# Reordering key and query preparation in a windowed attention plus feed-forward kernel on one Trainium2 core

## The chip, the cores and the metric

One Trainium2 chip (trn2), one core. The metric is the device time of one execution in microseconds (us). TensorE (PE) multiplies, VectorE (DVE), ScalarE (ACT) and GpSimd (POOL) work on its results, SyncE (SP) issues transfers; GpSimd also issues transfers, those that change the number type.

## The reference, cut to what matters

```python
# q, k, v: (4 batches, 8 heads, 768 positions, 64), fp32
k_sum = k.reshape(B, H, 24, 32, D).max(axis=3)        # one key per block of 32
v_sum = v.reshape(B, H, 24, 32, D).mean(axis=3)
scores_l = q @ k.T / 8     # kept where |i - j| < 16
scores_s = q @ k_sum.T / 8 + log(32)
a = softmax(concat(masked scores_l, scores_s))
x = a @ concat(v, v_sum)                              # (3072 tokens, 512)
h = x @ w_in                                          # 512 -> 2048
out = (h * sigmoid(1.702 * h)) @ w_out                # 2048 -> 512
```

## The kernel before, in words

The four batches go through one pipeline. While the feed-forward part of batch b runs on TensorE, the keys, queries and values of batch b + 1 are prepared and its attention is done in the gaps that the plans name. Every instruction of an engine is kept in program order, so the place of a call in the code is its place in the engine's queue.

Attention. For a head pair p (four of them, `NP`), `kx[p][s]` holds the keys turned (head dimension on the partitions), with 16 halo positions on each side and the 24 block keys in every tile of 128; s is the slot, b % 2. `qT` holds the turned queries. `scores(b, half, p)` does 12 products into a two-bank PSUM buffer of the pool `psb` (two buffers, tag "big") and one exponential on ScalarE; `mask(half, p)` multiplies by the window on VectorE; `values` multiplies with the value tile `vw[s]`, whose halos (`halo_dmas`) and block sums (`sum_dmas`, after `vsum` on TensorE and `block_sums` on VectorE) come by transfers within the chip. `norm` writes `x2`; its turned form `xT` feeds the feed-forward part.

Turning is done in two ways. `q_late(p)`, `tk` and `tq` turn on TensorE through PSUM and copy out. For batches 2 and 3, `xk(g, s)` turns two head pairs of keys with two transfers on SP, `xq(g, s)` two pairs of queries with one, `dx(half, g)` the attention result, one of four tiles `xT00` to `xT11`. They all stand in SP's queue, with the stores of the result and the halo and sum transfers.

Loads are issued by GpSimd. `load_turned` loads key or query groups (two transfers each for g = 0 and 1) into `kb` or `qb`, which have two buffers each; `load_batch(b)` issues the keys, 12 value transfers, and the queries (for batch 3 the queries are issued later, behind a small copy `gate2` that makes GpSimd wait for `xT11`). `rest_k` finishes keys: block maxima on VectorE, halos and block keys on VectorE or, out of `tk`, on GpSimd.

Feed-forward. Batch 0 is treated in two halves (`ff_in`, `ff_out`); in `ff_out(0, ...)` twelve slots follow each other and `plan0` names what comes beside each: `q0` to `q3` are `q_late`, `s0` to `s3` are `scores` and `mask` of the second half, `v`, `x` values and turns. Slots of batch 1 (`plan1`) run beside `ff_out(1, ...)`.

From batch 1 on the loop over b runs 16 first-layer steps in eight groups (n // 2 = 0 to 7: products `ph`, an activation on ScalarE, sums `g_sums` on VectorE) and then 21 second-layer products (`seq`, slots i = 0 to 20), seven for each of three token tiles t, with `plan` beside them. `product(b, t, what)` adds into banks A, B and C of the pool `pmm` (four buffers, tag "mm"). Bank A of a tile is kept open over products 1, 6, 7 and 4, and is read in between. Results go to `o1` and `o2` of a tile, taken from the pool `outp` (three buffers), and are stored by SP once written. In batch 1's pass these slots hold, in SP's order: tile 0's two stores, `xT00`, tile 1's `o1`, `xT01`, tile 1's `o2`, `xT10`, `xT11`, then the four key transposes of batch 3, tile 2's stores.

The last batch has a form of its own behind that (`ff_product`, `ff_copy`), which the change does not touch.

Of the kernel before, what the change touches and what calls it, by code (L numbers as in the profile page):

```python
# [35 lines left out]
def kernel(  # L36
# [28 lines left out]
    dve = _Ordered(tc, nc.vector)  # L65
    act = _Ordered(tc, nc.scalar)
# [14 lines left out]
    kb2, qb2 = {}, {}  # L81
# [41 lines left out]
    def load_turned(x, b, t2, name, gs_=(0, 1)):  # L123

        for g in gs_:
            t2[g] = castp2.tile([128, 2, NJ, 2, D], BF16, name=name, tag=name)
            for hh in range(2):
                h0 = hh * NP + 2 * g
                pool.dma_start(out=t2[g][:, :, :, hh].rearrange("p i a d -> p (i a) d"),
                               in_=x[b, h0:h0 + 2].rearrange("h (a p) d -> p (h a) d", p=128))  # L130

    def load_v(b):
        w5 = vw[b % 2].rearrange("p (j e) h c -> p j e h c", e=2)
        src = v[b].rearrange("h (j e p) d -> e j p h d", e=2, p=64)
        for j in range(NJ):
            for e in range(2):
                pool.dma_start(out=w5[e * 64:e * 64 + 64, j, e, :, 0:D], in_=src[e, j])
# [108 lines left out]
    def load_batch(b):  # L246
        if b == 3:
            pool.tensor_copy(out=gate2, in_=qTs[0][:, 0, 0:1])
        load_turned(k, b, kb2, "kb")
        if b == 3:  # L250
            pool.tensor_copy(out=gate2, in_=qTs[0][:, NP - 1, 0:1])
        if b == 1:
            load_turned(q, b, qb2, "qb", (0,))
        load_v(b)
        if b < 3:
            load_turned(q, b, qb2, "qb", (1,) if b == 1 else (0, 1))
# [12 lines left out]
    def copy(eng, out, in_):  # L269
        if eng is act:  # L270
            act.activation(out=out, in_=in_, func=ACT.Copy)
        elif eng == "dve_alone":

            dve.tensor_reduce(out=out, in_=in_.unsqueeze(len(in_.shape)), axis=AX.X, op=ALU.max)
        else:
            eng.tensor_copy(out=out, in_=in_)
# [65 lines left out]
    def at(ap, start, dims):  # L342
        a = ap[:, start:start + 1]
        return bass.AP(tensor=a.tensor, offset=a.offset, ap=[a.ap[0]] + dims)

    def flat_kx(p, s):
        return kx[p][s].rearrange("p t c -> p (t c)")
# [25 lines left out]
    def turn_plain(ps, src):  # L373

        n, rows = src.shape[0], src.shape[2]
        for r in range(rows):
            for h in range(2):
                pe.transpose(out=ps[h * 64:h * 64 + 64, r * n:r * n + n], in_=src[:, h, r],
                             identity=ident[0:n, 0:n])
# [31 lines left out]
    def turn_tiles(ps, src, n):  # L411

        for a in range(n):
            pe.transpose(out=ps[:, a * 128:a * 128 + 128], in_=src[:, a].rearrange("p h d -> p (h d)"),
                         identity=ident)

    def q_late(p, eng):
        if p != 2:
            ps = psb.tile([128, 2048], BF16, name="ps_q", tag="big")
        else:  # L420
            ps = pmm.tile([128, 1024], BF16, name="ps_q", tag="mm")
        turn_plain(ps[:, 0:HALF], qb2["late"][:, 2 * p:2 * p + 2])
        copy(eng, qT[p][0][:, HALF:S].rearrange("p (c r) -> p c r", r=JH),
             ps[:, 0:HALF].rearrange("p (r c) -> p c r", r=JH))
# [130 lines left out]
    def tk(p, s, eng):  # L555
        ps = psb.tile([128, 2048], BF16, name="ps_t", tag="big")[:, 0:S]
        turn_tiles(ps, kb2[p // 2][:, p % 2], NJ)
        copy(eng, at(flat_kx(p, s), 0, [[256, NJ], [192, 2], [1, 64]]),
             ps.rearrange("p (j e c) -> p j e c", e=2, c=64))
        rest_k(p, s, pool)  # L560

    def tq(p, s, eng):
        ps = pmm.tile([128, 1024], BF16, name="ps_t", tag="mm")[:, 0:S]
        turn_tiles(ps, qb2[p // 2][:, p % 2], NJ)
        copy(eng, qT[p][s], ps)

    def xk(g, s):
        k4 = kxs[s].rearrange("p i (j e) c -> p (i j) e c", e=2)
        src = kb2[g].rearrange("p i a h d -> p (i a h d)")
        for e in range(2):  # L570
            sp.dma_start(out=k4[:, 2 * g * NJ:2 * (g + 1) * NJ, e, e * 64:e * 64 + 64],
                         in_=src[e * 64:e * 64 + 64], transpose=True)
# [5 lines left out]
    def rest_k(p, s, eng=dve):  # L578
        ks = attp.tile([128, nb], BF16, name="ks", tag="ks")
        dve.tensor_reduce(out=ks.rearrange("p (j e n) -> p j e n", e=2, n=2),  # L580
                          in_=at(flat_kx(p, s), 0, [[256, NJ], [192, 2], [block, 2], [1, block]]),
                          axis=AX.X, op=ALU.max)
        key_halos(p, s, eng)
        key_rows(p, s, ks, eng)
# [92 lines left out]
    def ff_one(half, nt):  # L677
        ph = pmm.tile([128, HALF], F32, name="ph", tag="mm")
        ff_step(ph, half, nt)
        gelu(half, nt, ph)  # L680
# [13 lines left out]
    def w_sum(what, part):  # L694

        n = NT // 2
        c = slice(part * n // 2, (part + 1) * n // 2)
        w1, w2 = w_out_sb[:, 0:n], w_out_sb[:, n:]
        b11, b12, b21, b22 = w1[:, c, 0:N1], w1[:, c, N1:], w2[:, c, 0:N1], w2[:, c, N1:]
        a, b = {0: (b12, b11), 1: (b22, ws[:, 0, c]), 2: (b22, b12), 3: (b21, ws[:, 1, c])}[what]  # L700
        dve.tensor_tensor(out=ws[:, what, c], in0=a, in1=b, op=ALU.subtract)
# [14 lines left out]
    def win_sum(what):  # L716

        n = NT // 2 * 128
        k1, k2 = w_in_sb[:, K1], w_in_sb[:, K2]
        a11, a12, a21, a22 = k1[:, :, 0:n], k2[:, :, 0:n], k1[:, :, n:], k2[:, :, n:]  # L720
        a, b_, op = {0: (a21, a22, ALU.add), 1: (wsi[0], a11, ALU.subtract),
                     2: (a11, a21, ALU.subtract), 3: (a12, wsi[1], ALU.subtract)}[what]
        dve.tensor_tensor(out=wsi[what], in0=a, in1=b_, op=op)
# [167 lines left out]
    def exp_soon():  # L891
        act.activation(out=gate[:, 1:2], in_=gate[:, 0:1], func=ACT.Exp)
# [134 lines left out]
    load_batch(1)  # L1027


    plan0 = {1: ["q0", "q1", "q2"], 2: ["q3", "s0", "s1"], 4: ["s2", "s3"], 6: ["v0", "v1"], 8: ["x0"], 9: ["x1"]}  # L1030

    plan1 = {-1: ["s00", "s01"], 1: ["t2", "m00", "m01"], 2: ["t3", "s02"], 3: ["s03", "m02"], 4: ["m03", "s10"],
             5: ["s11", "m10"], 6: ["v00", "m11", "s12", "s13"], 7: ["v01", "g"], 8: ["m12", "m13"],
# [41 lines left out]
    def value_rows(s):  # L1075
        w5 = vw[s].rearrange("p (j e) h c -> p j e h c", e=2)
        halo_dmas(w5, 0)
        vsum(s)
        block_sums()
        sum_dmas(w5, 0)  # L1080
# [13 lines left out]
    for i, (ms, part) in enumerate((ms, part) for part in range(4) for ms in range(JH)):  # L1094
        ff_out(0, ms, part)
        beside0(i)
        if i in (10, 11):
# [2 lines left out]

    todo = {3: [lambda: tk(0, 1, act)], 4: [lambda: w_sum(2, 0)], 5: [lambda: tk(1, 1, act)],
            6: [lambda: w_sum(2, 1)], 7: [lambda: w_sum(3, 0)], 8: [lambda: tk(2, 1, act)], 
            10: [lambda: w_sum(3, 1)], 9: [lambda: tq(0, 1, dve)], 11: [lambda: tk(3, 1, act)], 12: [lambda: tq(1, 1, dve)],
            15: [lambda: value_rows(1)]}
    ff_in(1, range(3))
    for nt in range(3, NT):
# [15 lines left out]
    for b in range(1, B - 1):  # L1122
        nxt = b + 1 < B
        s = (b + 1) % 2
        if b == B - 2:
            for w in range(4):
                win_sum(w)
        for n in range(0, NT, 2):
            if n == 0:
                ff_open(order2[0:4], (lambda: tx(1, 1)) if b == 1 else None)  # L1130
            elif n == 2:
                for nt in order2[0:4]:
                    ff_one(1, nt)
                g_sums(0)
                g_sums(1)
            else:
                for nt in order2[n:n + 2]:
                    for half in range(2):
                        ff_one(half, nt)
                g_sums(n // 2, dve, (0, 1) if n + 2 == NT else (0, 1, 2, 3))  # L1140
            if nxt:
                if n == 0 and b > 1:
                    pool.tensor_copy(out=gate2, in_=xTT[1][1][:, 1, 0:1])
                    load_turned(q, b + 1, qb2, "qb")
                if n // 2 == 1:
                    value_rows(s)
                if n // 2 == 2 * b:
                    xq(0, s)
                    xq(1, s)
                if n // 2 in (2, 3, 4, 5):  # L1150
                    rest_k(n // 2 - 2, s)
        if nxt:
            exp_soon()
            beside(b + 1, -1)
        i = 0
        for t, what in seq:
            product(b, t, what)
            if i == 0:
                g_sums(NT // 2 - 1, dve, (2, 3))
            if nxt:  # L1160
                beside(b + 1, i)
            i += 1
            if nxt and b + 2 < B:
                if i == 1:
                    load_batch(b + 2)
                if i in (16, 18):
                    xk(i // 2 - 8, b % 2)

    mid.close()
    for ab in (True, False):  # L1170
# [1 line left out]
    b, n = B - 1, NT // 2  # L1172
# [79 lines left out]
```

## Time and profile before

| | |
|---|---|
| median of 3 runs | 206.19 us (205.59 to 206.76) |
| the profiled execution | 205.72 us |
| its span, first to last instruction | 203.7 us |
| PE busy / weight loads | 196.8 us / 136.7 us |
| DVE / ACT / POOL busy | 141.6 / 125.4 / 90.3 us |
| mean granted TensorE clock | 0.998 |
| moved by transfers | 28.13 MB, mean 138 GB/s |

All times in the views are from the start of the span. A row of a timeline gives start, length, engine, line, operation, what is written and read, a count and, in brackets, the idle time before it and what ended it. All program lines show as L28, a helper, so groups are told apart by the names of their tiles: `ps_q` are query turns of batch 0, `ps_s` scores, `ph` first-layer and `po` second-layer products. SPq and the POOL rows named DMA are the issue of transfers and not the transfers; these are told by their time from issue to landing. In rows of queues q0 is what GpSimd issued and q1 what SP and ACT issued: packets, MB, and the time that the packets took as a share of 16 transfer engines over the stretch (packets overlap, so it can pass 100%).

### The profile page before, as it was taken

How to read it: one execution, taken by the hardware profiler on the slowest of the kernel's cores; microseconds unless marked ns; L12 is line 12 of the kernel's file. 1: busy time of each engine (PE TensorE's matmuls, PEld its weight loads, DVE VectorE, ACT ScalarE, POOL GpSimd, SP SyncE). 2: the span in 40 equal slices, each digit the busy share in tenths (PEclk: the TensorE clock that was granted, in tenths of full speed). 3: DMA queues.
4: the chain of work that ended last, by engine and by line, in shares of the span. 5: the costliest groups of instructions: out<-in, count | busy, mean ns of one | idle time of the engine just before them, and what ended most of it. 6: DMA issues, size and time to landing. Idle time of an engine off the chain costs nothing.

```text
span 203.7 us, 5850 instructions
## 1 busy us (share of the span) xinstructions
PE 196.8 (97%) x2358; PEld 136.7 (67%) x2358; DVE 141.6 (70%) x391; ACT 125.4 (62%) x240; POOL 90.3 (44%) x141
## 2 busy tenths in 40 slices
PE   6899999999999999999999999998999999999993
PEld 6567554556754665665888965666888855668882
DVE  6776885594855874897768689895769567758221
ACT  4674875539777617777871546778580568984220
POOL 7955489456899592002974035000000019870000
PEclk9999999999999999999999999999999999999999
DMA  6999999999999999999999979999022940000223
GB/s 179 159 164 204 207 210 218 184 156 240 107 157 149 185 181 165 139 162 156 118 185 146 154 125 137 130 241 180 0 106 52 172 140 3 0 0 0 106 105 103
DMA packets 95994, 28.13 MB, mean 138 GB/s; under 512 B 83664, under 2 KB 93152, under 8 KB 95968
## 3 DMA queue, kind: packets, MB, share of 16 engines
q0 software_dynamic: 69648, 13.24, 82.1%
q1 hardware_dynamic: 26176, 14.39, 34.9%
q8 instruction: 18, 0.29, 0.6%
q10 hardware_dynamic: 144, 0.13, 0.2%
q14 instruction: 8, 0.07, 0.1%
HBM read 27.26 MB, written 6.29 MB: 165 GB/s over the span
## 4 chain that ended last, share of the span: by engine, by line
PE 82%; DMA 9%; DVE 5%; ACT 1%; issue 1%; SPq 0%; ACTq 0%; DVEq 0%
PE ph L28 23%; PE poA L28 16%; PE po L28 11%; PE poB L28 8%; PE ps_av L28 4%; PE phA L28 4%; DMA out_dram<-osb 4%; PE poC L28 4%; PE ps_s L28 3%; DMA qT<-qb 3%; DMA gT<-in_k_dram 2%; DVE ks L28 2%; PE ps_t L28 1%; PE ps_x L28 1%; DVE qT L28 1%; DVE gs L28 1%
## 5 line engine op out<-in xcount | busy, mean ns | idle before, releaser
L28 PE MATMUL ph<-xT,w_in_sb 128*128 128x384 f16 x400 | 67.6, 326 | 0.1
L28 PEld LDWEIGHTS <-w_in_sb 128*128 128x128 f16 x442 | 42.7, 98 | 27.1 <-issue 0.2
L28 ACT ACTIVATE gT<-ph 128x384 f16<-128x384 f32 x100 | 47.9, 492 | 17.9 <-PE ph L28 17.1
L28 PEld LDWEIGHTS <-gT 128*128 128x128 f16 x312 | 28.8, 98 | 11.0
L28 ACT ACTIVATE a_sb<-ps_s 128x768 bf16<-128x768 f32 (+1 forms) x32 | 25.0, 826 | 12.1 <-PE ps_s L28 12.1
L28 PEld LDWEIGHTS <-gs 128*128 128x128 f16 x288 | 27.7, 98 | 3.4
L28 POOL DMA_DIRECT2D vw<-in_v_dram x36 | 24.6, 704 | 11.2 <-DMA kb<-in_k_dram 4.1
L28 POOL TENSOR_TENSOR gs<-gT 128x384 f16<-128x384 f16 x8 | 7.3, 911 | 43.1 <-PE phC L28 42.0
L28 PE MATMUL po<-w_out_sb,gT 128*128 128x512 f16 x96 | 23.6, 380 | 0.0
L28 DVE TENSOR_TENSOR a_sb<-a_sb,mk 128x768 bf16<-128x768 bf16 x28 | 14.9, 554 | 6.5 <-ACT a_sb L28 5.9
L28 PE MATMUL poA<-ws,gs 128*128 128x256 f16 x144 | 18.7, 273 | 0.0
L28 DVE TENSOR_TENSOR x<-ps_av,rc 128x384 f16<-128x384 f32 x32 | 17.8, 558 | 1.1
L28 DVE TENSOR_TENSOR gs<-gT 128x384 f16<-128x384 f16 (+1 forms) x34 | 13.3, 390 | 7.2 <-ACT gT L28 6.9
L28 POOL DMA_DIRECT2D qb<-in_q_dram x16 | 15.1, 964 | 3.1 <-DMA v0n<-in_v_dram 1.7
L28 PEld LDWEIGHTS <-kx 64*128 64x128 bf16 (+1 forms) x378 | 10.0, 95 | 7.8 <-issue 4.9
L28 DVE TENSOR_REDUCE ks<-kx 128x24 bf16<-128x768 bf16 x12 | 11.4, 948 | 3.4 <-ACT kx L28 3.2
L28 POOL DMA_DIRECT2D kb<-in_k_dram x14 | 13.6, 987 | 0.3 <-issue 0.3
L28 ACT ACT_TABLE_LOAD x10 | 12.8, 1283 | 1.0 <-PEq L1236 0.8
L28 ACT ACTIVATE osb<-poA 128x256 f32<-128x256 f32 x9 | 3.5, 384 | 15.8 <-PE poA L28 15.8
L28 ACT ACTIVATE s<-poA 128x256 f32<-128x256 f32 x11 | 4.2, 385 | 11.2 <-PE poA L28 11.2
L28 PEld LDWEIGHTS <-a_sb 128*64 128x64 bf16 (+2 forms) x400 | 7.8, 108 | 2.8 <-issue 1.3
L28 PE MATMUL poA<-w_out_sb,gT 128*128 128x256 f16 x72 | 9.4, 273 | 0.0
(117 smaller groups left out, 288.9 us busy)
## 6 DMA issues: line engine op xcount, KB each, us to landing
out_dram<-osb SPq DMA_DIRECT2D x22, 256.0 KB, 3.7
kb<-in_k_dram POOLq DMA_DIRECT2D x14, 192.0 KB, 6.6
qb<-in_q_dram POOLq DMA_DIRECT2D x12, 192.0 KB, 10.3
vw<-in_v_dram POOLq DMA_DIRECT2D x36, 64.0 KB, 5.5
w_out_sb<-in_moe_w_out_dram POOLq DMA_DIRECT2D x4, 512.0 KB, 13.0
w_in_sb<-in_moe_w_in_dram POOLq DMA_DIRECT2D x3, 512.0 KB, 12.8
vw<-vs SPq DMA_DIRECT2D x6, 198.0 KB, 6.7
gT<-in_k_dram SPq DMA_DIRECT2D x2, 384.0 KB, 3.5
```

The lines of the kernel that those rows point to most:

```text
L28: r = f(*a, **kw)
```

## The change

Four places move, and no arithmetic changes.

```diff
-        load_turned(k, b, kb2, "kb")
+        load_turned(k, b, kb2, "kb", (1,) if b == 2 else (0, 1))
...
     def q_late(p, eng):
-        if p != 2:
+        if p < 2:
             ps = psb.tile([128, 2048], BF16, name="ps_q", tag="big")
         else:
             ps = pmm.tile([128, 1024], BF16, name="ps_q", tag="mm")
...
-    plan0 = {1: ["q0", "q1", "q2"], 2: ["q3", "s0", "s1"], 4: ["s2", "s3"], ...
+    plan0 = {1: ["q0", "q1", "q2"], 2: ["s0", "s1", "q3"], 4: ["s2", "s3"], ...
...
-            ... 11: [lambda: tk(3, 1, act)], ...
+            ... 11: [lambda: load_turned(k, 2, kb2, "kb", (0,)), lambda: tk(3, 1, act)], ...
...
-                if n // 2 == 2 * b:
+                if n // 2 == 2:
                     xq(0, s)
                     xq(1, s)
...
-                if i in (16, 18):
-                    xk(i // 2 - 8, b % 2)
+                if i in (8, 10):
+                    xk(i // 2 - 4, b % 2)
```

- Batch 2's first key group is loaded ahead of the turn of key pair 3 of batch 1 (`tk(3, 1, act)`), whose four halo copies stand behind it in GpSimd's queue; `load_batch(2)` then loads the second group only.
- The fourth late query pair of batch 0 is turned behind the score groups s0 and s1 and not ahead of them, and uses a buffer of `pmm` in place of one of `psb`. Its copy on VectorE stands behind the two masks.
- Batch 3's query transposes come at group 2 of batch 2's first layer and not at group 4 (for b = 1 both read group 2). SP issues nothing between these groups, so its order does not change there.
- Batch 3's four key transposes come after slots 8 and 10 of batch 1's second layer and not after 16 and 18. SP's order there becomes: tile 0's two stores, the four key transposes, `xT00`, tile 1's `o1`, `xT01`, tile 1's `o2`, `xT10`, `xT11`, tile 2's stores.

More of the change, by code (lines that the diff above doesn't have):

```diff
@@ L1027 @@
     load_batch(1)
-    plan0 = {1: ["q0", "q1", "q2"], 2: ["q3", "s0", "s1"], 4: ["s2", "s3"], 6: ["v0", "v1"], 8: ["x0"], 9: ["x1"]}
+    plan0 = {1: ["q0", "q1", "q2"], 2: ["s0", "s1", "q3"], 4: ["s2", "s3"], 6: ["v0", "v1"], 8: ["x0"], 9: ["x1"]}
     plan1 = {-1: ["s00", "s01"], 1: ["t2", "m00", "m01"], 2: ["t3", "s02"], 3: ["s03", "m02"], 4: ["m03", "s10"],
@@ L1102 @@
             6: [lambda: w_sum(2, 1)], 7: [lambda: w_sum(3, 0)], 8: [lambda: tk(2, 1, act)],
-            10: [lambda: w_sum(3, 1)], 9: [lambda: tq(0, 1, dve)], 11: [lambda: tk(3, 1, act)], 12: [lambda: tq(1, 1, dve)],
+            10: [lambda: w_sum(3, 1)], 9: [lambda: tq(0, 1, dve)], 11: [lambda: load_turned(k, 2, kb2, "kb", (0,)), lambda: tk(3, 1, act)], 12: [lambda: tq(1, 1, dve)],
             15: [lambda: value_rows(1)]}
```

## The prediction

> **What bounds the kernel now.** I read the page's busy shares first, then PE's own idle gaps, then the stretches around the moved lines: PE, VectorE (DVE) and ScalarE (ACT) near 33 us, SyncE's queue (SP) and GpSimd's (POOL) from 95 to 142 us, and the transfers beside them.
>
> ```profile
> PE 196.8 (97%) x2358; PEld 136.7 (67%) x2358; DVE 141.6 (70%) x391; ACT 125.4 (62%) x240; POOL 90.3 (44%) x141
> ```
>
> TensorE is busy all but 6.9 us of the span, so only its gaps can be won, and a new gap is paid in full. In the timeline two gaps lie at the changed lines. The first is in slot 2 of `plan0`:
>
> ```profile
> 33.08 0.36 PE L28 MATMUL ps_q<-wide,qb 128*64 128x128 bf16 x6
> 33.37 0.35 PE L28 MATMUL ps_s<-qT,kx 64*128 64x64 bf16 x12
> 34.09 0.35 PE L28 MATMUL ps_s<-qT,kx 64*128 64x64 bf16 x12 [0.37 <-DVE qT L28]
> 34.38 1.90 PE L28 MATMUL po<-w_out_sb,gT 128*128 128x512 f16 x8
> 36.21 0.52 PE L28 MATMUL ps_s<-qT,kx 64*128 64x64 bf16 x24
> ```
>
> The second is ahead of the last batch's scores:
>
> ```profile
> 140.83 0.53 PE L28 MATMUL ps_s<-qT,kx 64*128 64x64 bf16 x24 [0.55 <-DMA qT<-qb]
> ```
>
> **Part 1, the fourth late query pair behind two score groups.** VectorE's four query copies and its masks, and ScalarE's exponentials, each in its timeline:
>
> ```profile
> 31.89 2.15 DVE L28 COPY qT<-ps_q 128x384 bf16<-128x384 bf16 x4 [1.79 <-PE ps_q L28]
> 34.74 1.19 DVE L28 TENSOR_TENSOR a_sb<-a_sb,mk 128x768 bf16<-128x768 bf16 x2 [0.69 <-ACT a_sb L28]
> ```
>
> ```profile
> 33.82 1.51 ACT L28 ACTIVATE a_sb<-ps_s 128x768 bf16<-128x768 f32 x2 [1.95 <-PE ps_s L28]
> ```
>
> The copies end at 34.04, one each 0.54, and s1 starts at 34.09: it waits for the fourth copy, because q3 holds the `psb` buffer that s1 needs. With q3 in `pmm` and behind s0 and s1, TensorE does s0, s1 and q3 from 33.08 on without a wait: first and second copies are done by 33.0, and q3's `pmm` buffer is free once q2 is copied, at 33.5. The three cost 0.23 + 0.23 + 0.29 = 0.75 us instead of 34.38 - 33.08 = 1.30: 0.5 us won. (0.23 is half of the pair at 36.21; the next row, unquoted, starts 0.46 after it.) What is late next: q3's copy is now queued on VectorE behind the masks m0 and m1. s0 ends near 33.5, its exponential and s1's take 1.51 to 35.1, m1 ends 0.56 later at 35.65, q3's copy at 36.2. TensorE reaches s2 at 33.85 + 1.83 = 35.7 and s3 at 35.9, and s3 needs q3: a new wait of 0.3. Net 0.2 us won; bounds 0 (the exponentials start later) and 0.5 (the mask order does not hold up the copy). The value products at 38.5 keep their place behind the masks of s2 and s3, which move with TensorE.
>
> **Part 2, two key loads of batch 2 ahead of pair 3's key turn.** GpSimd issues four such loads in one go, and the score group that needs pair 3's halos is this one on PE:
>
> ```profile
> 59.32 4.05 POOL L28 DMA_DIRECT2D kb<-in_k_dram  x4
> ```
>
> ```profile
> 62.49 0.35 PE L28 MATMUL ps_s<-qT,kx 64*128 64x64 bf16 x12
> ```
>
> Two of the loads, 2.03 us, now precede pair 3's four halo copies, which end at 59.4 now and at 61.4 then, 1.1 us before TensorE needs them. The loads themselves start 1.06 us sooner, and the keys they feed are only transposed from 69.7 on. Priced at nothing, between 0 and 0.3 us of loss through the bus they share with the block sums' transfers.
>
> **Part 3, queries of batch 3 transposed at group 2 instead of 4.** SP does nothing else between those groups, so its order is the same; the two transposes still wait for their data. Zero by itself.
>
> **Part 4, four key transposes of batch 3 moved from slots 16 and 18 to 8 and 10.** This decides. SP's timeline:
>
> ```profile
> 103.13 2.61 SPq L28 DMA_DIRECT2D out_dram<-osb  x2
> 110.23 1.23 SPq L28 DMA_TRANSPOSE xT<-x  x1
> 112.25 0.33 SPq L28 DMA_DIRECT2D out_dram<-osb  x1
> 112.67 2.52 SPq L28 DMA_TRANSPOSE xT<-x  x1
> 115.28 0.53 SPq L28 DMA_DIRECT2D out_dram<-osb  x1
> 115.92 2.59 SPq L28 DMA_TRANSPOSE xT<-x  x2
> 119.08 6.78 SPq L28 DMA_TRANSPOSE kx<-kb  x4
> 125.97 1.19 SPq L28 DMA_DIRECT2D out_dram<-osb  x2
> 127.33 3.97 SPq L28 DMA_DIRECT2D vw<-vw  x4
> 131.41 2.45 SPq L28 DMA_DIRECT2D vw<-vs  x2
> 134.24 5.91 SPq L28 DMA_TRANSPOSE qT<-qb  x2
> ```
>
> The gain: today the four transposes keep SP for 6.78 us, the stores, halos and sums behind them are late, and they share the bus with the query loads (120.22 and 121.03 on POOL), so the query transposes start at 134.24 and the first lands as the scores start. With the keys gone from here the stores can go at about 119.4, the halos behind them, and the sums as soon as `block_sums` is done, about 127.4. The query loads themselves come later than today, for they wait on POOL for `xT11`, which the keys push from 120.2 to about 122 (worked out below): issued from 123 to 127, the first pair has landed by 131 with the landing times of the key loads below, and a transpose issued then, with SP's 5.91 for the pair, is through by 137. The scores need it at 140.1, so the 0.55 us goes whole.
>
> ```profile
> 120.22 0.72 POOL L28 CAST gate<-xT 128x1 bf16<-128x1 f16 x1 [10.98 <-DMA xT<-x]
> 121.03 4.07 POOL L28 DMA_DIRECT2D qb<-in_q_dram  x4
> ```
>
> The cost: the transposes are issued from 105.8, when SP ends its second store. Their keys are there: POOL issues the loads from 95.58 on, the last a microsecond before 99.63, and they land at most 6.7 later (the second row below, from the view of that tile).
>
> ```profile
> 95.58 4.05 POOL L28 DMA_DIRECT2D kb<-in_k_dram  x4 [0.27 <-issue]
> ```
>
> ```profile
> DMA to landing us min/median/max: 4.4/5.9/6.7
> ```
>
> They then stand ahead of `xT00` (110.23) and of the store of tile 1's `o1` (112.25). `outp` has three buffers, so tile 2's `o2` takes the buffer which that store must have emptied; its first write is VectorE's at 117.19, and TensorE's last product of the tile overwrites the bank that this write reads:
>
> ```profile
> 117.19 0.42 DVE L28 TENSOR_TENSOR osb<-poA,s 128x256 f32<-128x256 f32 x1 [0.45 <-PE poA L28]
> ```
>
> ```profile
> 117.81 1.04 PE L28 MATMUL poA<-ws,gT 128*128 128x256 f16 x8
> 118.68 5.36 PE L28 MATMUL ph<-xT,w_in_sb 128*128 128x384 f16 x32
> ```
>
> Today the store lands at 116.3 (4.1 after issue, first row below; an undisturbed one took 2.0, second row). TensorE waits if it lands after 117.81 - 0.42 - 0.05 - 0.2 (part 1) = 117.1, microsecond for microsecond. When does it land? SP's issue is not the limit (4 x 1.7 + 1.2 after 105.8 is 113.8, before its turn). The transfers are:
>
> ```profile
> out_dram<-osb SPq DMA_DIRECT2D x1, 256.0 KB, 4.1
> ```
>
> ```profile
> out_dram<-osb SPq DMA_DIRECT2D x1, 256.0 KB, 2.0
> ```
>
> ```profile
> q0 software_dynamic: 3337, 0.42, 220.8%
> ```
>
> ```profile
> q1 hardware_dynamic: 1313, 0.33, 70.3%
> ```
>
> ```profile
> q0 software_dynamic: 1835, 0.23, 86.1%
> q1 hardware_dynamic: 1571, 0.46, 81.3%
> ```
>
> ```profile
> q0 software_dynamic: 2344, 0.29, 124.0%
> ```
>
> These are packets per queue in four stretches: 64 to 67 us (GpSimd's loads alone, 1,110 per us), 119.9 to 123 (key transposes alone, busy 70.3% of 3.1 us: 602 per us of busy time), 72.1 to 76.3 (both), 108.2 to 112 (loads still to come there). The times add: 1835/1110 + 1571/602 = 4.3 us where the stretch took 4.2. A key transpose is 128 x 12 x 64 elements of 2 bytes, 768 packets of 256 B; `xT00` as much. From 108.2, when the two stores ahead are about through: loads 2344/1110 = 2.1, keys 3072/602 = 5.1, `xT00` 1.3, the store itself 0.2 to 2.3 (2.0 and 4.1 less 1.8 from issue to first packet: the soonest of the four key transposes landed 3.1 after its issue, in the row below, less 768/602), of which I take 0.7, as nothing contends by then. Sum 117.4: 0.3 us after the limit. `xT00` at 116.7 still meets 118.68; `xT01`, a store and the last two follow at 1.3 and 0.7 apiece, to 122, and the first products that read them run from 121.3 and 123.9 (half of that row of 5.36 and all of it). Bounds of this term: 0, and 4.0 (below).
>
> ```profile
> DMA to landing us min/median/max: 3.1/5.9/9.3
> ```
>
> The Trainium skill ("DMA: Bandwidth & Descriptors", Latency and other measured facts) gives 261 GB/s for a DMA transpose with a non-contiguous middle dimension. By that, keys and `xT00` would take 3.8 us instead of 6.4 and part 4's cost would be nil; the 0.33 MB in 70.3% of 3.1 us above are 151 GB/s, so this trace disagrees where keys are moved.
>
> **Sum.** -0.2 - 0.55 + 0.3 = -0.45 us. The profiled execution took 205.72 (span 203.7 and 2.0 around it), which gives 205.3; it lay 0.47 under the median of the runs, 206.19, which gives 205.75, rounded 205.8.
>
> **Rivals.**
>
> *The late store.* The transposes' packets go at the pace seen at 119.08, 6.78/4 = 1.7 us each with the next behind: keys 6.8 and `xT00` 1.7 make 118.8 with the loads, the store's 0.7 makes it 119.5, and its upper bound of 2.3 makes 121.1. The decisive point is a landing at 117.85, where the new stall eats the 0.75 won. At 120 the stall is 2.9 and the run 206.19 - 0.75 + 2.9 = 208.3; span of this case 207.8 to 209.4. For it: that store already took 4.1 in a quiet stretch. Against it: the additive check.
>
> *No stall at all.* This row counts packets from 139 to 142 us:
>
> ```profile
> q1 hardware_dynamic: 2620, 0.65, 97.1%
> ```
>
> Query transposes go at 900 per us of busy time. If the keys do too, keys and `xT00` take 4.3 us, the store lands at 115.3 and -0.75 remains: 205.4; with part 1's upper bound, 205.1. For it: the packets are of one size. Against it: the 602 measured on keys. The Trainium skill's figure above sits on this side.
>
> *The queries stay late.* The query loads wait on POOL for `xT11` (120.22), which follows the keys; were it to slip by three microseconds more than the two counted, or were the loads to land 14 us after issue, the 0.55 stays: +0.1, 206.3. Against it: today the loads share the bus with the four key transposes and with halos and stores that then lie behind them.
>
> **How the numbers follow.** Forecast 0.47, late store 0.25, no stall 0.20, queries late 0.08. About 0.5%, 1.03 us, is what a measurement of this kernel can tell from no change. Over 0.5% faster (under 205.16) needs the no-stall case with part 1 at its upper bound or the scatter of the runs (205.59 to 206.76): half of that case and a sixth of the forecast, 0.18. Slower (over 207.22) is nearly all of the late store, 0.22. The rest is 0.60. The range takes in the upper bounds of the gains and 0.2 of scatter, 204.9, and reaches to the late store's middle, 208.2.
>
> **What would show it.** Right: no wait of `ps_s` on a query copy near 34, a wait of about 0.3 before s3; SP's four key transposes at 106 to 113; query transposes by 132; no gap at the last batch's first scores. Wrong: a gap on TensorE before tile 2's last product over 1 us, with VectorE's `osb` write idle on a DMA; the 0.55 gap still there; or key transposes that SP starts only after 110.

## The result, and the profile after

The changed kernel took 207.40 us, the median of 14 executions (206.26 to 209.63); the kernel before, on the same chip, 206.38 (205.36 to 208.19). The ratio is 1.0054, with a 95% interval of 1.0028 to 1.0079: slower, by about 1.1 us, where 0.4 us less was forecast. The ratios, here and below, leave out executions over 1.5% above the fastest of their kernel, so a ratio and its two medians need not agree.

The profiled execution of the changed kernel took 206.67 us (span 204.7) and is one of the better ones. Its first part, PE in the timeline at the score groups of batch 0 (start, length, what is written and read, and in brackets the idle time before it and what ended it):

```profile
34.07 0.52 PE L28 MATMUL ps_s<-qT,kx 64*128 64x64 bf16 x24
34.53 0.36 PE L28 MATMUL ps_q<-wide,qb 128*64 128x128 bf16 x6
34.82 1.90 PE L28 MATMUL po<-w_out_sb,gT 128*128 128x512 f16 x8
36.65 0.35 PE L28 MATMUL ps_s<-qT,kx 64*128 64x64 bf16 x12
37.15 0.35 PE L28 MATMUL ps_s<-qT,kx 64*128 64x64 bf16 x12 [0.15 <-DVE qT L28]
```

The wait on the fourth query copy is gone and a smaller one stands before s3. SP's queue, then, and PE around tile 2's last product and at the last batch's scores:

```profile
107.20 6.36 SPq L28 DMA_TRANSPOSE kx<-kb  x4
113.69 1.52 SPq L28 DMA_TRANSPOSE xT<-x  x1
115.31 1.26 SPq L28 DMA_DIRECT2D out_dram<-osb  x1
...
132.07 5.79 SPq L28 DMA_TRANSPOSE qT<-qb  x2
```

```profile
119.14 1.03 PE L28 MATMUL poA<-ws,gT 128*128 128x256 f16 x8
120.01 5.63 PE L28 MATMUL ph<-xT,w_in_sb 128*128 128x384 f16 x32
...
141.81 0.52 PE L28 MATMUL ps_s<-qT,kx 64*128 64x64 bf16 x24
```

The keys are transposed early, the store of tile 1's `o1` is issued at 115.31, TensorE meets no gap at 119.14 and none at 141.81. The store lands 3.2 after issue, at 118.5, which is just in time: TensorE's product comes 0.92 after the one before it, where the others of the tile are 0.87 apart. By this profile the change looks harmless. The span is 1.0 us longer, and that much was lost in the first microseconds, where nothing was changed; behind them the gains at 34 and 141 (0.2 and 0.6) and two small new delays (0.5 near 67, 0.3 near 123) cancel. At the start the second key turn waits for a load:

```profile
7.33 0.53 PE L28 MATMUL ps_k<-wide,kb 128*64 128x128 bf16 x12 [0.99 <-ACT kb L28]
```

In the profile before it waited 0.32, at 6.34; in the later profiles from nothing to 1.04, whatever the kernel. A second execution of the same changed kernel, 209.85 us (span 207.8), shows what this one does not. SP, VectorE, PE, and the store's time from issue to landing:

```profile
106.10 7.64 SPq L28 DMA_TRANSPOSE kx<-kb  x4
...
115.76 0.52 SPq L28 DMA_DIRECT2D out_dram<-osb  x1
```

```profile
out_dram<-osb SPq DMA_DIRECT2D x1, 256.0 KB, 4.5
```

```profile
120.39 0.42 DVE L28 TENSOR_TENSOR osb<-poA,s 128x256 f32<-128x256 f32 x1 [3.46 <-DMA out_dram<-osb]
```

```profile
120.87 1.21 PE L28 MATMUL poA<-ws,gT 128*128 128x256 f16 x8 [2.71 <-DVE osb L28]
121.87 6.91 PE L28 MATMUL ph<-xT,w_in_sb 128*128 128x384 f16 x32
```

The store lands at 115.8 + 4.5 = 120.3. VectorE, which must write into the buffer that it empties, waits 3.46 us for it, and TensorE 2.71 for VectorE: the late store of the rivals. The next 32 products then take 6.91 us where they took 5.36, another 1.55. The windows of one microsecond show why; the third column from the end is the granted TensorE clock, the last the GB/s moved:

```profile
120.00:121.00 1.00, 0.13 (x2) 0.12 (x2) 0.61 (x2) 0.00 (x0) 0.00 (x0) 1.00 0.98 324
...
122.00:123.00 1.00, 1.00 (x5) 0.48 (x4) 0.97 (x2) 0.38 (x1) 0.00 (x0) 0.50 1.05 296
...
124.00:125.00 1.00, 1.00 (x4) 0.45 (x3) 1.00 (x2) 0.00 (x0) 1.00 (x2) 0.50 0.61 93
125.00:126.00 1.00, 1.00 (x7) 0.59 (x6) 0.81 (x1) 0.76 (x2) 1.00 (x2) 1.00 0.71 117
```

After the gap the clock is granted at half until 125, for 3.4 us by the trace. Of the changed kernel's 15 executions in all, three, at 208.8 to 209.9, had a mean clock of 0.990 to 0.992; the rest had 0.998 or more.

### The profile page after: what moved, and what is told of

Its sections match the earlier page's. It is cut to its first block, busy times and chain, and to the rows that moved or that the text cites. A ratio compares the mean times of both kernels' runs of the same rounds, so it can differ in the third digit from the quotient of the medians.

```text
span 204.7 us, 5852 instructions
## 1 busy us (share of the span) xinstructions
PE 197.2 (96%) x2358; PEld 136.8 (67%) x2358; DVE 141.2 (69%) x391; ACT 125.4 (61%) x240; POOL 91.7 (45%) x141
## 4 chain that ended last, share of the span: by engine, by line
PE 81%; DMA 9%; DVE 5%; ACT 2%; issue 1%; SPq 1%; ACTq 0%; DVEq 0%
PE ph L28 29%; PE poA L28 15%; PE poB L28 7%; PE po L28 7%; PE ps_av L28 4%; PE phA L28 4%; PE poC L28 4%; DMA vw<-vs 3%; DMA xT<-x 3%; DMA gT<-in_k_dram 2%; PE ps_s L28 2%; DVE ks L28 2%; PE ps_x L28 1%; DVE qT L28 1%; PE phB L28 1%
```

## The experiments

The kernel before took, in the same series: 206.06 (33 runs) beside each part by itself, 206.15 (29) beside the store on another queue, the filler and the first run with two transposes early, 206.15 (23) beside its second run and the one without value loads, 205.86 (11) beside the plain copies.

**Each part by itself.** Part 1 alone: `plan0` and the buffer of `q_late` as in the change, the rest as before.

```diff
-        if p != 2:
+        if p < 2:
...
-    plan0 = {... 2: ["q3", "s0", "s1"], ...
+    plan0 = {... 2: ["s0", "s1", "q3"], ...
```

> The kernel before with part 1 alone: the fourth late query pair turned behind s0 and s1, in a pmm buffer. All theories: TensorE wins 0.55 us at 33 to 34 and loses 0.15 to 0.3 to a wait ahead of s3, net 0.2 faster (ratio 0.999), unless the gain is swallowed by the wait for the query transposes of batch 3, which stays here: then the ratio is 1.000 and that wait grows from 0.55 to about 0.75. Start theory (the profile after lost its 1.0 us in the first 8 us, nothing else changed): the same.

Measured: 206.43, ratio 0.9988 (0.9954 to 1.0023).

Part 2 alone: one key group of batch 2 loaded ahead of `tk(3, 1, act)`.

> The kernel before with part 2 alone: two of batch 2's key loads ahead of pair 3's halo copies. Sums theory (the earlier loads delay the second block-sum transfer of batch 1, which the first value products wait for): a wait of ps_av on vw<-vs of 0.3 to 1.0 us near 66, vw<-vs landing 7 us after issue in place of 5.4, ratio 1.002 to 1.005. Turned-results theory (part 4 is the cost): no more than 0.3 us, ratio 1.000 to 1.001. Start theory: 1.000.

Measured: 206.04, ratio 1.0004 (0.9977 to 1.003). Between them these two profiles settle three small points. In part 1's, the wait before s3 is the one of the changed kernel (first row). The first profile after has a wait of 0.33 at the first value products of batch 1, near 67 us, put down to a late block-sum transfer; part 2 might have caused it, by its loads, but part 2 alone has none there. Part 1 alone has 0.32, but the profile with a filler below, without parts 1 and 2, has 0.47, and four with part 1 have none, the second of the changed kernel among them: the wait comes and goes and is not shown to be the change's. And neither profile has a gap at the last batch's scores, though both transpose the keys late, as before (second row part 1 alone, third row part 2 alone).

```profile
37.07 0.35 PE L28 MATMUL ps_s<-qT,kx 64*128 64x64 bf16 x12 [0.15 <-DVE qT L28]
```

```profile
141.60 0.52 PE L28 MATMUL ps_s<-qT,kx 64*128 64x64 bf16 x24
```

```profile
141.13 0.52 PE L28 MATMUL ps_s<-qT,kx 64*128 64x64 bf16 x24
```

In both, TensorE comes there later than before, by 1.3 us (part 1 alone) and 0.8 (part 2 alone) against the 140.28 at which it would have started without its wait, while the query transpose that the scores need lands at 140.5 and 140.9, before at 140.7. Both were 0.9 behind at 16 us, ahead of anything that was changed, part 1 alone with a wait of 1.04 like the one in the row at 7.33 above. So in these profiles the 0.55 that part 4 was to win is there only in the execution that starts up early.

Part 4 alone:

```diff
-                if i in (16, 18):
-                    xk(i // 2 - 8, b % 2)
+                if i in (8, 10):
+                    xk(i // 2 - 4, b % 2)
```

> The kernel before with part 4 alone: batch 3's key transposes in slots 8 and 10. Turned-results theory (xT11 lands 2 to 3 us later than its first product wants it): a gap of ph on xT of 0.3 to 1.5 us near 122, no gap at the last scores, ratio 1.000 to 1.005. Sums theory (part 2 is the cost): 0.55 won, 0.3 lost, ratio 0.997 to 0.999. Late-store rival of the prediction: the gap is at tile 2's last product, VectorE idle on a DMA before osb, 0.7 to 3 us.

Measured: 207.89, ratio 1.0103 (1.0066 to 1.0139); profiled execution 209.57, span 207.6. PE and VectorE in its timeline:

```profile
120.64 1.03 PE L28 MATMUL poA<-ws,gT 128*128 128x256 f16 x8 [2.53 <-DVE osb L28]
121.50 7.04 PE L28 MATMUL ph<-xT,w_in_sb 128*128 128x384 f16 x32
```

```profile
120.16 0.42 DVE L28 TENSOR_TENSOR osb<-poA,s 128x256 f32<-128x256 f32 x1 [3.28 <-DMA out_dram<-osb]
```

The loss is part 4's: late store, gap of 2.5 and slow products as in the second execution of the whole change. Without part 2:

> The changed kernel without part 2. Sums theory: no wait of ps_av near 66, and the time is that of the kernel before or 0.2 to 0.5 us under it, ratio 0.997 to 1.000. Turned-results theory: still slower, ratio 1.002 to 1.005. Start theory: within 0.2% of the kernel before.

Measured: 207.64, ratio 1.0064 (1.0031 to 1.0097); its profiled execution (211.7) had a gap of 3.51 at the same product, and its clock was at half for 6.8 us, which cost another 2.7. Parts 1 and 4 make the result without part 2.

**The changed kernel once more**, for a second profile.

> The changed kernel once more, for a second profile. Late-store theory: the gap ahead of tile 2's last product is there in some executions and not in others, 0.5 to 3 us, and grows with the time from the key loads' issue to the key transposes being short; if over 2 us, a lowered clock behind it. Turned-results theory: a gap of ph on xT of 0.3 us or more and none on the store.

Measured: 209.85; the rows are those above.

**The store on another queue.** All parts, and tile 1's `o1` of batch 1 is stored from ScalarE's queue, so it needn't stand behind the transposes on SP.

```diff
-            store("o1", t * 128, hi if last else slice(0, d_model))
+            store("o1", t * 128, hi if last else slice(0, d_model), act if b == 1 and t == 1 else sp)
```

> The changed kernel with one store, tile 1's o1 in batch 1's pass, issued by ScalarE's queue in place of SP's. Late-store theory (what costs is that this store stands behind four key transposes and xT00 in one queue, and tile 2's o2 waits for its buffer): it lands by 116.5, no gap ahead of tile 2's last product, 1 to 2 us under the changed kernel, ratio to the kernel before 0.996 to 1.000. Turned-results theory (xT01 to xT11 late): no change against the changed kernel, ratio 1.004 to 1.010. Bus theory (it is the shared transfer engines, whatever the queue): it lands at 118 to 120 all the same.

Measured: 206.35, ratio 1.0005 (0.9971 to 1.0039). ScalarE's issue and the landing:

```profile
114.09 0.37 ACTq L28 DMA_DIRECT2D out_dram<-osb  x1
```

```profile
out_dram<-osb ACTq DMA_DIRECT2D x1, 256.0 KB, 5.1
```

Issued 1.2 us sooner than in the first profile after, the store still took 5.1 us, and landed at 119.2: a place in the queue is worth little when the transfers ahead are still under way. The loss is out of the time; a gain is not in it. Why it is out this profile does not show: it started up late, so that TensorE came to tile 2's last product at 119.7, 1.7 later than it would have in the second execution of the whole change, and even so VectorE waited 0.75 for the store.

**Work in the gap.** Part 4 alone, with 12 products of 128 x 512, whose result nothing reads, ahead of tile 2's last product.

> The kernel with part 4 alone, and ahead of tile 2's last product in batch 1's pass twelve products of 128x512 into an unused bank (2.5 us of work that nothing reads). Clock theory (a gap of 2.5 us also halves TensorE's granted clock for some 3 us, which costs 1.7 more): no slice of lowered clock, the products ph behind it back from 7.0 to 5.4 us, and the time under that of part 4 alone where that had the drop. Gap-alone theory (the clock is scatter): the time is that of part 4 alone or up to 1 us more, since the filler is longer than the gap of a usual run.

Measured: 208.37 (207.69 to 208.90), ratio 1.0106 (1.0071 to 1.0142). PE:

```profile
118.49 2.75 PE L28 MATMUL ps_j<-w_in_sb 128*128 128x512 f16 x12
...
121.95 5.36 PE L28 MATMUL ph<-xT,w_in_sb 128*128 128x384 f16 x32
```

The store is as late, but TensorE stays busy and the products behind take 5.36 again; all ten executions had a mean clock of 0.999 or more, where four of twelve of part 4 alone had 0.990 to 0.992. So the gap, not the late data, lowers the clock. The filler does not pay: it costs every execution what only some would lose.

**Two key transposes early, two late.** All parts, with slots 8 and 16.

```diff
-                if i in (8, 10):
-                    xk(i // 2 - 4, b % 2)
+                if i in (8, 16):
+                    xk(i // 8 - 1, b % 2)
```

> The changed kernel with two of the four key transposes in slot 8 and the other two left in slot 16. Late-store theory: SP is through with the two by 109.3, before xT00 is ready, the store lands at 116 to 117, no gap there; SP's late part is 3.4 us shorter, so the query transposes start near 132 and the 0.55 us gap at the last scores shrinks to 0 to 0.2: ratio 0.996 to 0.999. Bus theory: the two alone still move the store past its limit, ratio 1.001 to 1.004.

Measured: 205.35, ratio 0.9986 (0.9951 to 1.002). Once more:

> The same kernel as with two key transposes at slot 8 and two at slot 16, once more for a narrower interval. Theory of the late store: two transposes early leave the store in time and still clear SyncE's queue for the query transposes, so the 0.55 at the last scores and about 0.2 at part 1 are won: 0.5 to 0.7 under the kernel before, ratio 0.9965 to 0.998. Rival, that two early transposes still cost a part-time stall at tile 2's last product: no difference, ratio 0.999 to 1.003.

Measured: 205.76, ratio 1.0005 (0.9979 to 1.003). The store is issued sooner, and TensorE has no gap at tile 2's last product and none at the last scores. The second run's profile shows it best, for it started up as early as the profile before, where the last two rows were at 117.81 and at 140.83, behind the wait of 0.55 (SP and PE):

```profile
112.34 0.33 SPq L28 DMA_DIRECT2D out_dram<-osb  x1
```

```profile
117.91 1.04 PE L28 MATMUL poA<-ws,gT 128*128 128x256 f16 x8
...
140.32 0.52 PE L28 MATMUL ps_s<-qT,kx 64*128 64x64 bf16 x24
```

The loss is gone. A gain is not shown: both medians are 0.4 to 0.8 under those of before, but both intervals hold 1. No version tried is measurably faster than the kernel before.

**What makes the store late: the value loads?** The changed kernel without batch 3's twelve value loads.

```diff
-        load_v(b)
+        if b < 3:
+            load_v(b)
```

> The changed kernel with the twelve value loads of the last batch left out (its value products then read batch 1's values, so this run is read for its times alone). It takes one suspected cost off the transfers while the four early key transposes are under way. Shared-transfers theory: the value loads' packets are what pushes the store of tile 1's o1 from 117 to 119-120; without them the four keys, issued at 106 to 113, land by about 114, xT00 by 115, the store by 116 to 117; TensorE has no gap ahead of tile 2's last product, its next ph row takes the usual 5.4, and the run takes 205.0 to 205.6 (the profile before less the 0.55 at the last scores and about 0.2 of part 1). Rival, that the transposes themselves are slow when they follow one another on SyncE's queue (1.7 each, xT00 and the store behind them): the store still lands at 118.5 or later, with a gap of 1 or more and a time of 206.5 to 208.

Measured: 205.52, ratio 0.9982 (0.9947 to 1.0016), profiled span 203.0. SP, the store's landing and PE:

```profile
105.88 5.98 SPq L28 DMA_TRANSPOSE kx<-kb  x4
111.99 1.31 SPq L28 DMA_TRANSPOSE xT<-x  x1
113.40 1.28 SPq L28 DMA_DIRECT2D out_dram<-osb  x1
```

```profile
out_dram<-osb SPq DMA_DIRECT2D x1, 256.0 KB, 3.5
```

```profile
117.77 1.04 PE L28 MATMUL poA<-ws,gT 128*128 128x256 f16 x8
118.64 5.36 PE L28 MATMUL ph<-xT,w_in_sb 128*128 128x384 f16 x32
```

The key transposes, in the rows of issues from 106 to 114 us, land a median of 7.2 us after issue with the value loads beside them (second run of the changed kernel; 5.3 in the first) and 4.2 without:

```profile
kx<-kb SPq DMA_TRANSPOSE x4, 7.2
```

```profile
kx<-kb SPq DMA_TRANSPOSE x4, 4.2
```

The store is issued 2.4 us sooner, lands at 116.9 and not at 120.3, and gap and slow products are gone. The value loads are what the keys collide with; that they also take GpSimd's time, and not only the transfers', was not told apart.

**Or the transposing?** In the second run of the changed kernel two stretches of over a microsecond hardly move a byte, at 10 and 6 GB/s (last column of its windows), though keys and loads, then `xT00` and the store, are outstanding:

```profile
109.70:111.10 1.40, 1.40 (x15) 1.27 (x13) 1.33 (x5) 0.00 (x0) 0.00 (x0) 1.00 1.15 10
...
116.90:118.20 1.30, 1.26 (x12) 0.98 (x10) 0.03 (x1) 0.56 (x2) 0.00 (x0) 1.00 0.12 6
```

Here the four early key transposes are replaced by eight plain transfers of the same bytes, between the same tiles.

```diff
+    def xk_plain(g, s):
...
+        for e in range(2):
+            for u in range(2):
+                sp.dma_start(out=k4[u * 64:u * 64 + 64, 2 * g * NJ:2 * (g + 1) * NJ, e, e * 64:e * 64 + 64],
+                             in_=src[e * 64:e * 64 + 64, u * 2 * NJ * 64:(u + 1) * 2 * NJ * 64].rearrange("p (a c) -> p a c", c=64))
...
-                    xk(i // 2 - 4, b % 2)
+                    xk_plain(i // 2 - 4, b % 2)
```

> The changed kernel with batch 3's four early key transposes replaced by plain transfers of the same bytes between the same tiles (two for each, 64 partitions apiece, packets of 128 bytes), so batch 3's keys are not turned and the run is read for its times alone. In the profiles with early keys, two stretches of 1.3 to 1.8 us in which hardly a packet moves lie between the first key packet and the store of tile 1's o1 (109.7 to 111.1 and 116.9 to 118.2 in the second run of the changed kernel, at 10 and 6 GB/s). Theory that these pauses come with the transposes in flight: with plain copies there is no such stretch between 106 and 113, at most one later at xT00 or xT01; the store lands by 117.3, TensorE has no gap over 0.3 ahead of tile 2's last product, and the run takes 205.2 to 205.9. Rival, that it is the bytes and packets alone (0.4 MB more, twice the packets, beside the value loads): the store lands at 118.5 or later, with a gap of 1 or more and 206.8 to 208.

Measured: 207.67, ratio 1.0087 (1.0047 to 1.0126), span of the profiled execution 204.9. The same two windows, SP, the store's landing and PE:

```profile
109.70:111.10 1.40, 1.40 (x15) 1.25 (x14) 1.33 (x5) 0.00 (x0) 0.00 (x0) 1.00 1.72 165
116.90:118.20 1.30, 1.30 (x14) 1.16 (x13) 0.27 (x1) 0.80 (x2) 0.00 (x0) 1.00 0.85 244
```

```profile
106.34 7.98 SPq L28 DMA_DIRECT2D kx<-kb  x8
114.42 1.80 SPq L28 DMA_TRANSPOSE xT<-x  x1
116.32 0.53 SPq L28 DMA_DIRECT2D out_dram<-osb  x1
```

```profile
out_dram<-osb SPq DMA_DIRECT2D x1, 256.0 KB, 2.5
```

```profile
119.39 1.03 PE L28 MATMUL poA<-ws,gT 128*128 128x256 f16 x8 [0.99 <-DVE osb L28]
```

Half of each theory came out. The pauses are gone, from these windows and from all of 100 to 126 us, where each other profile with early key transposes has at least one of 0.6 us or more under 20 GB/s; and the store needs 2.5 us instead of 4.5. That the pauses belong to the transposes fits all thirteen traces. In the pauses shown, ten or more small packets that started just before take 1.0 to 1.8 us each; between 10 and 69.5 us, ahead of the first transpose by transfer, none of some 34,000 packets of up to 512 bytes in any trace takes over 0.8. A transpose does not always bring a pause, for here the four of `xT` go without. But eight transfers hold SP for 7.98 us, the store is issued at 116.3, and it is late by a microsecond all the same. Twice as many instructions on SP was a poor choice for this test: it put a second cause in place of the first.

## Why the prediction was wrong

**The step that failed** is the landing of tile 1's `o1` store. The prediction put it at 117.4, from an addition of packet times, with a limit of 117.1. The rule for the limit held: in the second run of the changed kernel the product would have started 0.87 after the one before it, at 117.99, which by the prediction's 0.47 for the write puts the limit at 117.5, and a landing at 120.3 makes a stall of 2.8; it was 120.87 - 117.99 = 2.9. The landing did not: 118.5 in the first run, 120.3 in the second, 120.0 with part 4 alone. The sum had no term for the two pauses. In the second run they are 1.4 and 1.3 us; 117.4 + 2.7 + 0.3 (SP began at 106.10, not 105.8) is 120.4. With part 4 alone they are 1.3 each, which makes 120.3. A pause could have been seen in the profile before, where the store that took 4.1 us "in a quiet stretch" sat in one:

```profile
114.70:116.00 1.30, 1.30 (x14) 1.17 (x13) 0.46 (x1) 0.79 (x3) 0.00 (x0) 1.00 0.34 19
```

That this store took twice the 2.0 of another was quoted, and answered by "nothing contends by then". The run without value loads has two as well:

```profile
108.90:109.80 0.90, 0.90 (x15) 0.81 (x10) 0.87 (x3) 0.00 (x0) 0.00 (x0) 1.00 0.78 20
113.90:115.10 1.20, 1.20 (x13) 1.08 (x12) 1.17 (x3) 0.47 (x2) 0.00 (x0) 1.00 0.71 17
```

For it the sum gives 117.4 - 2.1 (the loads) + 2.1 (the pauses) = 117.4, and 116.9 was measured. It is no exact tool: the first run after, which had one full pause of 1.0 and began its keys 1.4 late, comes to 119.8 and landed at 118.5. Nor was SP's issue out of play, as the prediction had it with the store's turn at 113.8. The store was issued at 115.31 and 115.76 in the two runs, with 6.36 and 7.64 us for the keys' issue, and at 113.40 with 5.98 where the value loads are left out; from 115.76 even the 2.0 of an undisturbed store ends at 117.8, past the limit. Whether slow transfers hold up the issue there, or the other way round, is not shown. And the keys' packet rate is no constant: in one microsecond of the first run after, while nothing but keys and `xT00` is under way, they go at 285 GB/s.

```profile
113.50:114.50 1.00, 1.00 (x32) 0.90 (x27) 0.86 (x4) 0.00 (x0) 0.00 (x0) 1.00 1.28 285
```

The Trainium skill ("DMA: Bandwidth & Descriptors", Latency and other measured facts) gives 261 GB/s for such a transpose; this stretch is nearer to it than to the 151 GB/s that the prediction took from the trace, and the four keys as a whole are still later than either rate says. The 602 packets per us behind these 151 came from a stretch in which SP issued a transpose of 768 packets every 1.7 us, 452 per us, and 424 per us went out, so it may have measured the issue and not the transfers.

**A term that was missing**: what a gap does to the work behind it. The formula of the late store priced it microsecond for microsecond; a gap of 2.5 or 2.7 also cost 1.55 to 1.7 in the products that follow (6.91 and 7.04 against 5.36), and the gap of 3.51 another 2.7. The filler shows that the gap is the cause. The Trainium skill ("TensorE: Matmul & The Clock Gate", Why this matters for your kernels) advises against idle gaps above some 3 us between bursts of products, because the clock then falls to half. The fall agrees with the windows above; the length doesn't quite, for 2.53 and 2.71 were enough here. The 0.99 with plain copies was not: the 32 products behind it take 5.36.

**A gain that was counted whole**: the 0.55 at the last scores. It was read from one profile, which started up early; two others with the keys late do not have it, and the second run with two transposes early, which started up early too, does win it. In an execution that starts up late, little more than part 1's 0.2 is left of the 0.75.

**What was right.** Part 1: the wait of 0.37 gone, the three groups through 0.55 sooner, a new wait of 0.15 before s3 (0.3 forecast) and 0.2 left over by the timeline; its time (0.9988) is too small a change to measure. Part 2: nothing. Part 3 was forecast at nothing by itself and was not run by itself. The query transposes start at 132.07 and the last scores do not wait, as forecast, with no time to show for it. The late store was named as a rival, at 208.3, with the stall that came, though it put the lateness down to 1.7 us for each transpose and not to pauses, and was given 0.25 where it was the usual case. A smaller miss: the first products that read `xT11` were put at 123.9, but the row of 32 products holds both halves, and in the first run they wait a little (5.63 for 5.36).

**The median.** The late store was in four of the five profiles with all four keys early on SP and the value loads beside them; the first profile after is the exception. It differs in two ways. It started up 1.0 late, so TensorE reached the product at 119.1 and not at 118.0; the queries' landing, above, did not follow such a delay. And GpSimd's loads began at 94.49 and SP's keys at 107.20, in the second run at 95.29 and 106.10: 1.9 us more between them, so that fewer value loads were left beside the keys, it had one full pause and not two, and the store landed 1.8 sooner. The run without value loads supports the second point, and so do the five profiles together: the last value load lands at 113.7, 115.4, 115.7, 115.9 and 116.4, and the store 4.4 to 4.8 us behind it in each. Neither point was tried by itself. The profiles show stalls of 0, 1.0 (with plain copies) and 2.5 to 3.5; that the usual execution at 207.4, with its clock undiminished, has one between them is argued and not shown. What starts a pause stays open.

## What to carry to other kernels

A transfer moved into a quiet stretch of its own queue can still collide with another queue's loads: look at what all queues have outstanding there, and at who waits for the buffer that the next store in line must empty. A gap read from one profiled execution can be a matter of how it started up: count it whole only when a second profile has it. And a gap on TensorE of a few microseconds is dearer than its length, so some of the work behind it is to be priced at half the clock.

## What the runs showed of the hardware that was not expected

- After a gap of 2.5 or 2.7 us TensorE's clock was granted at half for 3.4 us, so products that take 5.36 us took 6.9 to 7.0; with a gap of 3.5 it was at half for 6.8 us, from 1.1 before the gap's end. After the one gap of 1.0 us it was not.
- With transposes in flight, transfers of all queues at times paused for 0.9 to 1.4 us at 6 to 20 GB/s; with plain transfers of the same bytes in the same place they went on at 165 GB/s.
- The store of tile 1's `o1`, 256 KB, took 3.2 to 5.1 us where the transfers ahead of it were transposes, on SP's queue and on ScalarE's alike, and 2.5 where the keys were copied plainly; undisturbed stores took 2.0. In the kernel before, the two stores right behind the four late key transposes and beside the query loads took 8.2 and 8.5.
